# Linear attention with a gated block: the reciprocals of the heads' sums go through DRAM to q's rows

## The chip, the core and the metric

The kernel runs on one core of one Trainium2 chip. The metric is the time of one execution on the device, in microseconds (us). A TensorE (PE) does the products, VectorE (DVE), ScalarE (ACT) and GpSimd (POOL) do the rest; most transfers are issued from the queue of SyncE (SP), a few from POOL's. PSUM tiles hold products, SBUF tiles hold operands, DRAM holds inputs, outputs and scratch.

## The reference

S = 2048 rows, D = 576, 32 heads of 18 columns, an inner width of 4608 in the gated block. All is in f32.

```python
xn = layernorm(x)
q, k, v = heads(xn @ wqkv)                  # 32 heads of 18
phi = lambda t: where(t > 0, t + 1, exp(t)) + 1e-6
kv  = einsum("bhsd,bhse->bhde", phi(k), v)
z   = sum over s of phi(k)                  # the key sums
den = einsum("bhqd,bhd->bhq", phi(q), z) + 1e-6
o   = einsum("bhqd,bhde->bhqe", phi(q), kv) / den
s   = o @ wo
g   = silu((gelu(xn @ w_gate) * (xn @ w_up)) @ w_down)
out = x + s * g
```

## The kernel before

The rows are cut into four blocks of 512 (`TBN`), numbered `tb` = 0 to 3, and each block into four tiles of 128 (`TT`). An operand that must keep f32 precision is held as a high and a low word in f32r, and a product is several passes over those words (`PASSES`).

Stage 1 (to about 183 us): `kv_tile(t)` runs over the sixteen row tiles. It makes k, v and the last 64 columns of q for one tile in three products (`x_mm(t, 0)`, `(t, 1)`, `(t, 2)`), applies phi, and adds to the accumulators of kv and of the key sums (`kv_mm(t - 1)`). `q_turn(t)` turns those columns of q of two tiles with PE and copies them into `ph4[tb]`. The products q of blocks 0 and 1 lie in the middle of this stage (`q_store`): their phi is stored in DRAM (`ph_d`), to be loaded later (`q_load`).

Stage 2 (about 183 to 290 us) is the place of the change. q's columns are laid out in five groups: four groups `gi` of seven heads (126 columns and two columns that belong to the last head), and a fifth with what is left. Before the change it goes so:

- `q_hold(2, 7, ...)` and `q_hold(3, 8, ...)` do the four q products (14 passes each) of blocks 2 and 3; between them stand the pieces of work in their lists. `kv_done` masks kv; `kv_wo(gi)` multiplies kv by wo, so that s = phi(q) @ (kv wo) / den. The same product has two more columns of wo, one of ones, that give the key sums; `kv_wo` spreads them over heads into `zc`. `move_rows` copies the two odd rows into their places, with small copies from SBUF to SBUF.
- `den(tb)`: twenty products (in two passes each) of phi(q) with `zc` give the sums of the 32 heads for 512 rows, then 1e-6 is added and the reciprocal taken, on DVE; four ACT and four DVE steps put it as high and low words into `rd`.
- `scale(tb, ...)`: the reciprocals must stand on the rows of phi(q), 18 rows for each head. For each of the five groups, one product of the 0/1 matrix `sel` with `rd` puts them there in PSUM, and DVE multiplies phi(q) by it. `make_sel` and `copy_sel` make the matrix beforehand on POOL and ACT.
- `halve(tb, ...)`: high word on ACT, low word on DVE.
- `s_mm(tb, t)`: 28 passes make one row tile of s, ACT copies it, SP stores it in DRAM (`s_d`).

The tiles of s run in the order of blocks 2, 3, 0, 1; the table `aside` names the work after each tile: den, scale and halve of the next block, `build` of operands of the next stage (T1 to T4), `load_mat(0)` of the first weights and `back(...)`, which reads back other operands (B11, T2, T1) by POOL's queue. Nearly every instruction is pinned in program order on its engine (`pin`), DMA issues too, so each engine's list, SP's included, is the order of the code.

Stage 3 (about 290 to 1085 us) makes the gate and up products in matrices, and stage 4 the down products and the end.

Buffers are named slots: `big(i, ...)`, `mid(i, ...)`; a later tile in the same slot waits for the last use of the earlier one. `bank` gives one of six PSUM banks, `own_bank` one of two, `gl_tile` one of six SBUF tiles of 512 columns, `tmp` one of four.

Of the kernel before, what the change touches and what calls it, by code (L numbers as in the profile page):

```python
# [15 lines left out]
P = 128  # L16
# [39 lines left out]
def block_kernel(ctx, tc, x, xe, xt_d, wq_d, wkv0_d, wkv1_d, wkv2_d, wo, wgu_d, wd_d, out):  # L56
# [330 lines left out]
    pkv, pks, vas, es, pqt, ph4, ph, ph_d = ({} for _ in range(8))  # L387
# [69 lines left out]
    def q_turn(t):  # L457

        tb, i = divmod(t, TT)
        b = bank(f"qx_{t}")  # L460
        for n in range(2):
            pin(nc.tensor.transpose(b[:, n * P : (n + 1) * P], pqt.pop(t + n)[:, 0:2], ident))
        if i == 0:
            ph4[tb] = gl_tile([P, TBN], f"ph4_{tb}")
            if tb < 2:
                ph_d[tb] = dr.tile([P, NHG, TBN], F32, name=f"phd_{tb}")
        act(ph4[tb][:, i * P : (i + 2) * P], b[:, 0:P2], AF.Copy)
        if i == 2 and tb < 2:
            dma(out=ph_d[tb][:, 4, :], in_=ph4[tb])
# [41 lines left out]

    def q_store(tb, gi):
        o = gl_tile([P, TBN], f"ph_{tb}_{gi}")
        q_mm(tb, gi, o)
        dma(out=ph_d[tb][:, gi, :], in_=o)

# [6 lines left out]
    def ph_of(tb, gi):  # L523
        return ph4[tb] if gi == 4 and tb > 1 else ph[tb][:, gi, :]
# [48 lines left out]
    def load_wo():  # L573

        n = NHG * P
        t = big(14, [P, 2 * n + D + 2], F32, "kvm")
        at["one"] = t[0:H, n + D + 2 :].rearrange("p (g j) -> p g j", g=NHG)
        at["kvm"] = t[:, 0:n].rearrange("p (g j) -> p g j", g=NHG)
        at["wo"] = w = big(12, [P, 4, D + 2], F32, "wo_t")
        at["wo4"] = w4 = t[:, n : n + D + 2]  # L580
# [5 lines left out]
        dma(out=w4[1 : W4 + 1, 0:D], in_=wo[4 * GW : D, :])  # L586

    def kv_wo(gi):
# [8 lines left out]
        zc, mh = at["zc"], at["maskh"]  # L597
# [3 lines left out]
        for c, cs in enumerate((slice(0, HALF), slice(HALF, D + 2))):  # L601
            pw.append(bank(f"kw_{gi}_{c}"))
            mm(
                pw[c][0:wdt, 0 : cs.stop - cs.start], at["kvm"][0:k, gi, 0:wdt], w[0:k, cs],
                start=True, stop=True,
            )
        r, x_ = slice(0, Q4 if gi == 4 else GW), slice(Q4, W4)
        z = pw[1][:, HALF : HALF + 1]
# [6 lines left out]
        if gi == 4:  # L615
            vec("tensor_copy", zx[x_], z[x_])
# [3 lines left out]
        vec("tensor_scalar", zc[r, gi, :], mh[r, gi, :], z[r], None, op0=ALU.mult)  # L620
# [5 lines left out]
    def move_rows():  # L626
        for gi in range(4):
            r, e = slice(Q4 + 2 * gi, Q4 + 2 * gi + 2), slice(GW, P)
            dma(out=at["zc"][e, gi, H - 1 : H], in_=zx[r])
# [3 lines left out]
    def make_sel():  # L633

        n = NHG * P
        buf = big(15, [P, n + TBN], F32R, "aux")
        at["sel"] = sel = buf[:, 0:n].rearrange("p (g j) -> p g j", g=NHG)
        at["rd"] = rd = buf[:, n : n + TBN]
        one = at["one"]
        pool("memset", one, 1.0)  # L640
        four, last = one[:, 0:4, 0:GW], one[:, 4, :].rearrange("p (r j) -> p r j", r=2)
        for o, pattern, base in ((four, [[GW, 4], [1, GW]], 0), (last, [[0, 2], [1, Q4]], 4 * GW)):
            pool(
                "affine_select",
                out=o, in_=o, compare_op=ALU.is_ge, fill=0.0, base=base,
                pattern=pattern, channel_multiplier=-DH,
            )
            pool(
                "affine_select",
                out=o, in_=o, compare_op=ALU.is_ge, fill=0.0, base=DH - 1 - base,  # L650
                pattern=[[-s_, n_] for s_, n_ in pattern], channel_multiplier=DH,
            )
        pool(
                "affine_select",
            out=one[:, 0:4, GW:P], in_=one[:, 0:4, GW:P], compare_op=ALU.is_ge, fill=0.0,
            base=1 - H, pattern=[[0, 4], [0, P - GW]], channel_multiplier=1,
        )
        pool("memset", rd.bitcast(F32), 0.0)

    def copy_sel():  # L660
        one, sel = at["one"], at["sel"]
        for i in range(4):
            r = slice(i * H, (i + 1) * H)
            if i % 2:
                act(sel[r], one, AF.Copy)
            else:
                pool("tensor_copy", sel[r], one)

    HB = TBN // 4

    def den(tb):

        pd = bank(f"d_{tb}")
        for gi in range(NHG):
            for i in range(4):
                mm(
                    pd[H * i : H * (i + 1), 0:HB], at["zc"][:, gi, :],
                    ph_of(tb, gi)[:, i * HB : (i + 1) * HB],
                    start=(gi == 0), stop=(gi == NHG - 1),
                )  # L680
        r = gl_tile([P, HB], f"r_{tb}")
        rd = at["rd"]
        vec("tensor_scalar", r, pd[:, 0:HB], EPS, None, op0=ALU.add)
        vec("reciprocal", r, r)
        for i in range(4):
            c, rows, low = slice(i * HB, (i + 1) * HB), slice(H * i, H * (i + 1)), i ^ 1
            act(rd[rows, c], r[rows], AF.Copy)
            vec("tensor_sub", rd[H * low : H * (low + 1), c], r[rows], rd[rows, c].bitcast(F32))

    pqs, s_d, words = {}, {}, {}  # L690

    def scale(tb, *gs):

        for gi in gs:
            pb = bank(f"b_{tb}_{gi}")
            mm(pb, at["sel"][:, gi, :], at["rd"], start=True, stop=True)
            p = ph_of(tb, gi)
            vec("tensor_mul", p, p, pb)

    def halve(tb, *gs):  # L700

        if tb % 2 and gs[0] == 0:
            words[tb] = [big(i, [P, 4, TBN], F32R, f"pq_{tb}_{i}") for i in (12, 14)]
        for gi in gs:
# [7 lines left out]
            else:  # L712
                if tb % 2:
# [575 lines left out]
    for n in range(N0, 2 * N0):  # L1289
# [13 lines left out]
        if n == 2 * N0 - 2:  # L1303
            after.append(make_sel)
        if n == 2 * N0 - 1:
            after += [copy_sel, lambda: difference(1, 1), lambda: difference(1, 2)]
        kv_tile(n, early, middle, ends, after)

    q_hold(2, 7, [
        [lambda: kv_mm(2 * N0 - 1), kv_done, lambda: difference(1, 3)],  # L1310
        [lambda: q_turn(2 * N0 - 2), lambda: kv_wo(4)],
        [lambda: kv_wo(0), lambda: kv_wo(1), move_rows],
        [lambda: kv_wo(2), lambda: kv_wo(3)],
    ])
    q_hold(3, 8, [
        [lambda: den(2)],
        [lambda: scale(2, 0, 1), lambda: halve(2, 0, 1)],
        [lambda: scale(2, 2, 3), lambda: halve(2, 2, 3)],
        [lambda: scale(2, 4), lambda: halve(2, 4)],
    ])  # L1320
# [7 lines left out]
    def first_matrix():  # L1328
# [5 lines left out]
    q_load(0, 7)  # L1334
    aside = {
        (2, 0): [lambda: den(3), lambda: build(1, "T1", X_SLOT["T1"])],
        (2, 1): [lambda: scale(3, 0, 1), lambda: halve(3, 0, 1)],
        (2, 2): [lambda: scale(3, 2, 3, 4), lambda: halve(3, 2, 3, 4)],
        (2, 3): [lambda: build(1, "T3", X_SLOT["T3"]), lambda: load_mat(0), lambda: q_load(1, 8)],
        (3, 0): [lambda: den(0), lambda: build(1, "T2", X_SLOT["T2"])],  # L1340
        (3, 1): [lambda: scale(0, 0, 1), lambda: halve(0, 0, 1), lambda: back("B11")],
        (3, 2): [lambda: scale(0, 2, 3, 4), lambda: halve(0, 2, 3, 4)],
        (3, 3): [lambda: build(1, "T4", X_SLOT["T4"]), lambda: back("T2")],
        (0, 0): [lambda: den(1), lambda: mat_sums(0)],
        (0, 1): [lambda: scale(1, 0, 1), lambda: halve(1, 0, 1)],
        (0, 2): [lambda: scale(1, 2, 3, 4), lambda: halve(1, 2, 3, 4)],
        (0, 3): [lambda: back("T1")],
# [4 lines left out]
    for tb in (2, 3, 0, 1):  # L1352
# [82 lines left out]
```

## Time and profile before

| | |
|---|---|
| median of 3 runs | 1492.87 us (1492.6 to 1493.64) |
| the profiled execution | 1492.91 us, span 1491.2 us |
| granted TensorE clock | 1.000 |
| PE busy | 1481.9 us, 99% of the span |
| DVE, ACT, POOL busy | 71%, 38%, 36% |
| HBM | 174 GB/s over the span |

All the profile's times come from the one profiled execution and count from its first instruction. A row of the timeline or of the chain gives start, length, engine, what was written and what was read; "x14" counts instructions. A row of the windows view gives the stretch, its length, the busy time (and count) of PE, PEld (weight loads), DVE, ACT and POOL, then the granted clock, the DMA share and GB/s. A row of grouped instructions gives line, engine, operation, out<-in and shapes, count, then the summed busy time and the mean in ns, then the idle time before them. SPq is SP's queue of DMA issues: the length there is that of the issue, not of the transfer.

### The profile page before, as it was taken

Reading aid. Unit: us, or ns where it says so; the run is one execution under the profiler, and the core shown is the slowest. Engines: PE = TensorE matmul, PEld = TensorE weight load, DVE = VectorE, ACT = ScalarE, POOL = GpSimd, SP = SyncE. Lnnn points to the kernel's source line nnn. Section 1 sums busy time; section 2 is a strip of 40 time slices with the busy share of each in tenths; the row PEclk is TensorE's granted clock in tenths of the full one; section 3 lists DMA queues with packets and bytes.
Section 4 is the critical chain, followed back from the end, with each engine's and each line's share of the span. In section 5 each row is a group of like instructions: output and inputs, shape, how many; then the busy total and the mean of one; then the engine's idle time right before and its main releaser. Section 6 shows DMA issues by size and latency. Waiting matters only on the chain.

```text
span 1491.2 us, 22334 instructions
## 1 busy us (share of the span) xinstructions
PE 1481.9 (99%) x8355; PEld 1327.8 (89%) x8355; DVE 1063.9 (71%) x1586; ACT 560.9 (38%) x1043; POOL 543.6 (36%) x521
## 2 busy tenths in 40 slices
PE   9999999999999999999999999999999999999998
PEld 8989989988888888888888888888899999999998
DVE  7667577377788787788787778787785575555775
ACT  5535445332232232332222322223445454445443
POOL 5442431144665544565554565554310020001120
PEclk9999999999999999999999999999999999999999
DMA  6355015533443423444433344333697766686873
GB/s 238 131 213 180 1 43 194 206 149 132 165 173 144 162 106 132 149 174 152 157 119 122 143 173 171 138 134 119 216 335 252 235 215 220 226 292 217 299 253 113
DMA packets 114614, 260.67 MB, mean 175 GB/s; under 512 B 10234, under 2 KB 38778, under 8 KB 112458
## 3 DMA queue, kind: packets, MB, share of 16 engines
q1 hardware_dynamic: 112730, 249.95, 46.7%
q0 software_dynamic: 1632, 8.91, 1.6%
q8 instruction: 65, 1.06, 0.3%
q10 hardware_dynamic: 144, 0.39, 0.1%
q14 instruction: 43, 0.35, 0.1%
HBM read 161.27 MB, written 97.91 MB: 174 GB/s over the span
## 4 chain that ended last, share of the span: by engine, by line
PE 94%; DVE 2%; DMA 2%; ACT 1%; issue 0%; POOL 0%; SPq 0%; ACTq 0%; DVEq 0%; POOLq 0%
PE bd L1010 27%; PE al L804 15%; PE ga L804 15%; PE de L804 15%; PE be L804 8%; PE kv L93 6%; PE s L93 4%; PE q L93 2%; DMA kept_T<-xo_T 1%; PE kv_a L93 1%; ACT xo_T L87 0%; DMA xf_B<-in_xt_dram 0%; PE d L93 0%; PE kw L93 0%; DVE xo_T L90 0%
## 5 line engine op out<-in xcount | busy, mean ns | idle before, releaser
L1010 PEld LDWEIGHTS bd<-t,s 128*128 128x128 f32 x3024 | 400.9, 188 | 0.1
L1010 PE MATMUL bd<-t,s 128*128 128x288 f32 x3024 | 401.0, 295 | 0.0
L90 DVE TENSOR_TENSOR s<-sr,s 128x512 fp32r<-128x512 f32 x252 | 176.1, 739 | 119.8 <-ACT s L87 117.8
L87 ACT ACTIVATE s<-sr 128x512 fp32r<-128x512 f32 x252 | 149.1, 626 | 189.0 <-PE bd L1010 131.0
L96 POOL TENSOR_TENSOR hs<-h,h 128x512 f32<-128x512 f32 x68 | 94.7, 1401 | 203.8 <-DVE h L90 201.1
L87 ACT ACTIVATE h<-h 128x512 f32<-128x512 f32 x108 | 67.1, 633 | 244.5 <-POOL sm L96 123.1
L96 POOL TENSOR_TENSOR sx<-sx 128x288 f32<-128x288 f32 x24 | 27.9, 1180 | 322.9 <-DVE sx L90 321.8
L93 PE MATMUL kv<-wkv,xo_B 128*128 128x416 f32 (+1 forms) x672 | 129.9, 349 | 0.0
L93 PEld LDWEIGHTS kv<-wkv,xo_B 128*128 128x128 f32 x672 | 121.4, 188 | 1.3 <-POOL wkv L96 0.2
L90 DVE TENSOR_TENSOR wa<-raw,wa 128x256 fp32r<-128x256 f32 x72 | 79.2, 1100 | 50.8 <-ACT wa L87 47.5
L96 POOL TENSOR_TENSOR sm<-raw 128x384 f32<-128x384 f32 x72 | 75.8, 1053 | 107.1 <-DMA raw<-in_wgu_dram 86.5
L90 DVE TENSOR_TENSOR h<-h,u 128x512 f32<-128x512 f32 x108 | 95.7, 886 | 3.7
L87 ACT ACTIVATE wa<-sm 128x1152 fp32r<-128x1152 f32 x36 | 41.8, 1161 | 135.8 <-PE de L804 135.8
L90 DVE TENSOR_TENSOR wa<-sm,wa 128x768 fp32r<-128x768 f32 x72 | 63.1, 877 | 36.9 <-ACT wa L87 36.1
L96 POOL TENSOR_TENSOR td<-td 128x288 f32<-128x288 f32 x72 | 70.1, 973 | 53.0 <-DMA td<-in_wd_dram 48.7
L90 DVE TENSOR_TENSOR wb<-raw,wb 128x256 fp32r<-128x256 f32 (+1 forms) x108 | 72.0, 666 | 7.3 <-ACT wb L87 5.8
L90 DVE TENSOR_TENSOR wb<-sm,wb 128x256 fp32r<-128x256 f32 x72 | 61.3, 852 | 20.6 <-ACT wb L87 20.0
L87 ACT ACTIVATE u<-al 128x512 f32<-128x512 f32 x72 | 40.9, 592 | 88.4 <-PE al L804 88.4
L90 DVE TENSOR_TENSOR u<-u,ga 128x512 f32<-128x512 f32 x72 | 49.3, 686 | 19.9 <-PE ga L804 19.3
L804 PE MATMUL al<-xo_B,wa 128*128 128x512 f32 x252 | 63.0, 389 | 0.0
L804 PE MATMUL be<-xo_T,wa 128*128 128x512 f32 x252 | 63.0, 389 | 0.0
L804 PE MATMUL be<-xr_T,wa 128*128 128x512 f32 x252 | 63.0, 389 | 0.0
(175 smaller groups left out, 2773.4 us busy)
## 6 DMA issues: line engine op xcount, KB each, us to landing
sr<-hs SPq DMA_DIRECT2D x252, 256.0 KB
hs<-h SPq DMA_DIRECT2D x68, 512.0 KB
raw<-in_wgu_dram SPq DMA_DIRECT2D x36, 768.0 KB
hs<-hs SPq DMA_DIRECT2D x102, 256.0 KB
td<-in_wd_dram SPq DMA_DIRECT2D x18, 576.0 KB
td<-td SPq DMA_DIRECT2D x18, 576.0 KB
tr<-td SPq DMA_DIRECT2D x16, 576.0 KB
tr<-in_wd_dram SPq DMA_DIRECT2D x12, 576.0 KB
```

The source lines that it names most:

```text
L87: pin(nc.scalar.activation(*args, **kw))
L90: pin(getattr(nc.vector, op)(*args, **kw))
L93: pin(nc.tensor.matmul(*args, **kw))
L96: pin(getattr(nc.gpsimd, op)(*args, **kw))
L804: nc.tensor.matmul(o, w[0:rows, wi, :], xop[0:rows, xi, :], start=(start and n == 0), stop=(n == len(PASSES) - 1), skip_group_check=True,)
L1010: nc.tensor.matmul(banks[j][:, 0:HALF], hw[n, s][:, a, t * P : (t + 1) * P], w[:, c, g % 4], start=(new and g == 0 and m == 0), stop=(g == ...
```

## The change

The products with `sel` go, and with them `make_sel`, `copy_sel` and the words in `rd`. `den_end` stores the reciprocals of a block in DRAM (`rd[tb]`, 32 heads x 512), and `to_rows(tb)` copies them from there into an SBUF tile `rb[tb]` in the layout of phi(q), by nine transfers whose source repeats: four of 7 heads x 18 rows, one of two rows for four groups, and for the fifth group two of 3 heads x 18 rows and two of one head x 10 rows. `scale` multiplies by `rb`. There is one slot for `rb` (15), which the four blocks use in turn.

The key sums come from five products of two columns (`key_sums`), placed ahead of kv times wo. Blocks of s run in the order 0, 2, 3, 1: block 0 is loaded first, block 3 is stored and loaded again instead of held. `den` of block 0 lies between the q products of block 2, that of block 2 between those of block 3, that of block 3 is spread in five parts (`den_mm`) up to behind the first tile of s. `q_turn` in a row tile moves from behind the second product to behind the third.

```diff
@@ kv_tile
         x_mm(t, 1)
-        if t % 2 == 0 and t % (2 * TT):
-            q_turn(t - 2)
...
         x_mm(t, 2)
         run(list(middle))
+        if t % 2 == 0 and t % (2 * TT):
+            q_turn(t - 2)
@@ q_mm
-        phi(o, pq, f"q{tb}_{gi}", tb % 2 == 1)
+        phi(o, pq, f"q{tb}_{gi}", tb > 0)
@@ new
+    def key_sums():
+        pz = bank("z")
...
+            mm(
+                pz[0:wdt, 2 * gi : 2 * gi + 2], at["kvm"][0:k, gi, 0:wdt], w[0:k, D : D + 2],
+                start=True, stop=True,
+            )
+        x_ = slice(Q4, W4)
+        vec("tensor_copy", zx[x_], pz[x_, 8:9])
+        for gi in range(NHG):
...
+            vec("tensor_scalar", zc[r, gi, :], mh[r, gi, :], z, None, op0=ALU.mult)
+        for gi in range(4):
+            dma(out=zc[GW:P, gi, H - 1 : H], in_=zx[Q4 + 2 * gi : Q4 + 2 * gi + 2])
@@ den
+    def den_end(tb):
+        r = gl_tile([P, HB], f"r_{tb}")
+        vec("tensor_scalar", r, dens[tb][:, 0:HB], EPS, None, op0=ALU.add)
+        vec("reciprocal", r, r)
+        rd[tb] = dr.tile([H, TBN], F32, name=f"rd_{tb}")
+        dma(out=rd[tb].rearrange("h (i c) -> i h c", i=4), in_=r)
...
+    def to_rows(tb):
+        rb[tb] = o = big(15, [P, NHG, TBN], F32, f"rb_{tb}")
+        def heads(rows, gi, h, n, k):
+            src = rd[tb][h : h + n, None, :].to_broadcast([n, k, TBN])
+            dma(out=o[rows : rows + n * k, gi, :], in_=src)
+        for gi in range(4):
+            heads(0, gi, HG * gi, HG, DH)
+        src = rd[tb][H - 1 : H, None, :].to_broadcast([2, 4, TBN])
+        dma(out=o[GW:P, 0:4, :], in_=src)
+        for r in (0, Q4):
+            heads(r, 4, 4 * HG, 3, DH)
+            heads(r + 3 * DH, 4, H - 1, 1, Q4 - 3 * DH)
@@ scale
-            pb = bank(f"b_{tb}_{gi}")
-            mm(pb, at["sel"][:, gi, :], at["rd"], start=True, stop=True)
             p = ph_of(tb, gi)
-            vec("tensor_mul", p, p, pb)
+            vec("tensor_mul", p, p, rb[tb][:, gi, :])
@@ the order of stage 2
+    q_load(0, 7)
+    q_hold(2, 8, [
+        [lambda: kv_mm(2 * N0 - 1), kv_done],
+        [key_sums, lambda: q_turn(2 * N0 - 2), lambda: difference(1, 3)],
+        [lambda: den(0), lambda: to_rows(0), lambda: kv_wo(4)],
+        [move_rows, lambda: kv_wo(0), lambda: kv_wo(1)],
     ])
+    behind = [
+        [lambda: kv_wo(2), lambda: scale(0, 0, 1), lambda: halve(0, 0, 1)],
+        [lambda: kv_wo(3), lambda: den(2), lambda: scale(0, 2, 3), lambda: halve(0, 2, 3),
+         lambda: den_mm(3, 4, ph4[3], True, False), lambda: den_mm(3, 0, pg[0], False, False)],
+        [lambda: scale(0, 4), lambda: to_rows(2), lambda: halve(0, 4),
+         lambda: den_mm(3, 1, pg[1], False, False)],
+        [lambda: q_load(3, 7), lambda: den_mm(3, 2, pg[2], False, False)],
+    ]
+    for gi in range(4):
+        q_store(3, gi)
+        run(behind[gi])
...
+        (0, 0): [lambda: den_mm(3, 3, pg[3], False, True), lambda: den_end(3),
+                 lambda: build(1, "T1", X_SLOT["T1"])],
+        (0, 1): [lambda: scale(2, *five), lambda: halve(2, *five), lambda: to_rows(3),
+                 lambda: q_load(1, 8)],
+        (0, 3): [lambda: build(1, "T3", X_SLOT["T3"]), lambda: load_mat(0)],
+        (2, 0): [lambda: build(1, "T2", X_SLOT["T2"])],
+        (2, 1): [lambda: scale(3, *five), lambda: halve(3, *five), lambda: back("B11")],
+        (2, 2): [lambda: den(1), lambda: to_rows(1)],
+        (2, 3): [lambda: build(1, "T4", X_SLOT["T4"]), lambda: back("T2")],
+        (3, 0): [lambda: mat_sums(0)],
+        (3, 1): [lambda: scale(1, *five), lambda: halve(1, *five)],
+        (3, 3): [lambda: back("T1")],
```

More of the change, by code (lines that the diff above doesn't have):

```diff
@@ L386, in block_kernel @@
     left = {}
-    pkv, pks, vas, es, pqt, ph4, ph, ph_d = ({} for _ in range(8))
+    pkv, pks, vas, es, pqt, ph4, ph, ph_d, pg = ({} for _ in range(9))
     def x_mm(t, c, passes=None, new=bank):
@@ L464, in q_turn @@
             ph4[tb] = gl_tile([P, TBN], f"ph4_{tb}")
-            if tb < 2:
+            if tb != 2:
                 ph_d[tb] = dr.tile([P, NHG, TBN], F32, name=f"phd_{tb}")
         act(ph4[tb][:, i * P : (i + 2) * P], b[:, 0:P2], AF.Copy)
-        if i == 2 and tb < 2:
+        if i == 2 and tb != 2:
             dma(out=ph_d[tb][:, 4, :], in_=ph4[tb])
@@ L523, in ph_of @@
     def ph_of(tb, gi):
-        return ph4[tb] if gi == 4 and tb > 1 else ph[tb][:, gi, :]
+        return ph4[tb] if gi == 4 and tb == 2 else ph[tb][:, gi, :]
     def q_load(tb, i):
@@ L575, in load_wo @@
         n = NHG * P
-        t = big(14, [P, 2 * n + D + 2], F32, "kvm")
-        at["one"] = t[0:H, n + D + 2 :].rearrange("p (g j) -> p g j", g=NHG)
+        t = big(14, [P, n + D + 2], F32, "kvm")
         at["kvm"] = t[:, 0:n].rearrange("p (g j) -> p g j", g=NHG)
         at["wo"] = w = big(12, [P, 4, D + 2], F32, "wo_t")
-        at["wo4"] = w4 = t[:, n : n + D + 2]
+        at["wo4"] = w4 = t[:, n:]
         for t in (w, w4[:, None, :]):
@@ L586, in load_wo @@
         dma(out=w4[1 : W4 + 1, 0:D], in_=wo[4 * GW : D, :])
+    def key_sums():
+        pz = bank("z")
+        zc, mh = at["zc"], at["maskh"]
+        for gi in range(NHG):
+            wdt, k = (W4, W4 + 1) if gi == 4 else (GW, GW + 1)
+            w = at["wo4"] if gi == 4 else at["wo"][:, gi]
+            mm(
[4 more added lines that the diff above has]
+        vec("tensor_copy", zx[x_], pz[x_, 8:9])
+        for gi in range(NHG):
+            r = slice(0, Q4 if gi == 4 else GW)
+            z = pz[r, 2 * gi : 2 * gi + 1]
+            vec("tensor_scalar", zc[r, gi, :], mh[r, gi, :], z, None, op0=ALU.mult)
+        for gi in range(4):
+            dma(out=zc[GW:P, gi, H - 1 : H], in_=zx[Q4 + 2 * gi : Q4 + 2 * gi + 2])
     def kv_wo(gi):
@@ L600, in kv_wo @@
         pw = []
-        for c, cs in enumerate((slice(0, HALF), slice(HALF, D + 2))):
+        for c in range(2):
+            cs = slice(c * HALF, (c + 1) * HALF)
             pw.append(bank(f"kw_{gi}_{c}"))
             mm(
-                pw[c][0:wdt, 0 : cs.stop - cs.start], at["kvm"][0:k, gi, 0:wdt], w[0:k, cs],
+                pw[c][0:wdt, 0:HALF], at["kvm"][0:k, gi, 0:wdt], w[0:k, cs],
                 start=True, stop=True,
@@ L628, in move_rows @@
             r, e = slice(Q4 + 2 * gi, Q4 + 2 * gi + 2), slice(GW, P)
-            dma(out=at["zc"][e, gi, H - 1 : H], in_=zx[r])
             for t, i in ((at["kvh"], 2), (at["kvl"], 3)):
                 dma(out=t[e, gi, :].bitcast(F32), in_=at["kv4"][r, i, :].bitcast(F32))
[L633 to L646, printed above, removed]
-            )
[L648 to L669, printed above, removed]
+    HB = TBN // 4
+    rd, rb, dens = {}, {}, {}
+    def den_mm(tb, gi, src, first, last):
+        if first:
+            dens[tb] = own_bank(f"d_{tb}")
+        for i in range(4):
+            mm(
+                dens[tb][H * i : H * (i + 1), 0:HB], at["zc"][:, gi, :],
+                src[:, i * HB : (i + 1) * HB], start=first, stop=last, skip_group_check=True,
+            )
@@ L681, in den @@
[L681 to L688, printed above, removed]
+            den_mm(tb, gi, ph_of(tb, gi), gi == 0, gi == NHG - 1)
+        den_end(tb)
@@ L1302, in block_kernel @@
             after.append(lambda: difference(1, 0))
-        if n == 2 * N0 - 2:
-            after.append(make_sel)
         if n == 2 * N0 - 1:
-            after += [copy_sel, lambda: difference(1, 1), lambda: difference(1, 2)]
+            after += [lambda: difference(1, 1), lambda: difference(1, 2)]
         kv_tile(n, early, middle, ends, after)
[L1309 to L1313, printed above, removed]
-    ])
[L1315 to L1320, printed above, removed]
+    q_load(0, 7)
[4 more added lines that the diff above has]
+        [move_rows, lambda: kv_wo(0), lambda: kv_wo(1)],
+    ])
+    behind = [
[9 more added lines that the diff above has]
+        run(behind[gi])
     X_BACK = {"B11": 13, "T2": 7, "T1": 8, "T3": 12, "B21": 4, "B22": 5, "T4": 6}
@@ L1330, in first_matrix @@
         return mat_pieces(0)
-    q_load(0, 7)
+    five = range(NHG)
     aside = {
[L1336 to L1347, printed above, removed]
+        (0, 0): [lambda: den_mm(3, 3, pg[3], False, True), lambda: den_end(3),
[10 more added lines that the diff above has]
+        (3, 3): [lambda: back("T1")],
         (1, 0): [lambda: pieces.extend(first_matrix()), lambda: run(pieces[0])],
@@ L1351, in block_kernel @@
     pieces = []
-    for tb in (2, 3, 0, 1):
+    for tb in S_ORDER:
         for t in range(TT):
```

18 lines of the change are left out of this document (5 added, 13 removed).

## The prediction

> **What bounds the kernel now.** I read the page's shares first, then the chain of waits, then who waited for whom on PE, then the stage between 183 and 290 us in the chain's order of time.
>
> ```profile
> span 1491.2 us, 22334 instructions
> PE 1481.9 (99%) x8355; PEld 1327.8 (89%) x8355; DVE 1063.9 (71%) x1586; ACT 560.9 (38%) x1043; POOL 543.6 (36%) x521
> ...
> PE 94%; DVE 2%; DMA 2%; ACT 1%; issue 0%; POOL 0%; SPq 0%; ACTq 0%; DVEq 0%; POOLq 0%
> ```
>
> PE is busy for 99% of the span and is 94% of the chain that ended last. So an instruction taken from PE is time won, and a wait put into PE's list is time lost, one for one. The granted clock is 1.00 in every stretch quoted below, so the clock plays no part. In the stretch 120 to 300 us, the waits on PE are two:
>
> ```profile
> PE qx L462 <- POOL w_q L96: 1.1, 1, 1.1
> PE b L93 <- DVE aux L90: 0.2, 1, 0.2
> ```
>
> The stage itself, from the chain (start, length, what):
>
> ```profile
> 187.54 3.26 PE q L93 x14
> 190.80 0.22 PE qx L462 x2
> 191.02 0.97 PE kw L93 x4
> 192.00 3.20 PE q L93 x14
> 195.20 1.95 PE kw L93 x8
> ...
> 205.50 1.23 PE d L93 x40
> ...
> 210.14 0.47 PE b L93 x2
> ...
> 227.26 3.72 PE s L93 x28
> 230.98 0.69 PE b L93 x3
> ```
>
> A q product group takes 3.20 us, a den 1.23, a tile of s 3.72, and a reciprocal product b 0.23 (0.47/2, 0.69/3). DVE, ACT and POOL hide beside these.
>
> **What leaves PE.** Twenty products b go: 20 x 0.23 = 4.6 us. The 0.2 us wait before one of them goes too. q_turn moves behind the third x_mm of its tile, over 2 us later, longer than the 1.1 us that PE waited there for POOL; after it PE does kv_mm of the tile before, which had no wait. So 1.1 us goes.
>
> **What PE gains.** key_sums issues five products with two columns, f32, so ten passes. The trace has no such product. The passes of den cost 1.23/40 = 0.03 us, those of kw 1.95/8 = 0.24; so 0.3 to 2.4 us. I take 0.11 a pass, as in the two narrow transposes qx (0.22/2): 1.1 us. kw loses two columns of 290: nothing. den's products are the same number in other places. Sum on PE: -4.6 - 0.2 - 1.1 + 1.1 = -4.8 us. The dropped make_sel, copy_sel and the sixteen small aux steps lay on POOL, ACT and DVE under PE's work; they are worth nothing by themselves.
>
> **Waits that the change adds.** First, den(0) needs the key sums, which the four two-row copies carry into zc:
>
> ```profile
> 192.83 0.71 SPq L99 DMA_DIRECT2D small<-eps_t  x1
> ...
> 195.02 0.56 SPq L99 DMA_DIRECT2D small<-eps_t  x1
> ...
> 217.86 0.37 SPq L99 DMA_DIRECT2D ph<-phd  x1
> ```
>
> In the new PE list q(2,1) ends at 190.8 (old time scale), key sums end at 191.9, qx and q(2,2) at 195.3. The sums reach zx at about 192.1; four issues of at most 0.71 us end at 195, and den reads the groups in the same order. I put 0 for this wait, with 1 us as upper end.
>
> Second, and decisive: the new transfers. rb is 128 rows x 5 groups of 2 KB, sent four times. What transfers cost here:
>
> ```profile
> 143.00:144.00 1.00, 1.00 (x8) 1.00 (x7) 1.00 (x2) 0.10 (x1) 0.00 (x0) 1.00 0.88 341
> 218.80:222.90 4.10, 4.05 (x61) 3.46 (x59) 1.32 (x3) 1.35 (x3) 1.29 (x1) 1.00 0.84 322
> 222.90:223.10 0.20, 0.20 (x2) 0.20 (x3) 0.14 (x1) 0.00 (x0) 0.00 (x0) 1.00 0.00 0
> 223.20:223.90 0.70, 0.70 (x8) 0.70 (x7) 0.67 (x2) 0.00 (x0) 0.00 (x0) 1.00 1.00 392
> ```
>
> These are stretches of the windows view; the last two columns are the busy share of the 16 DMA engines and GB/s. Line two is ph's load of 1.31 MB, issued at 217.86, landed at 222.9: about 1 us of start, 4.1 of moving. Line four is a store of an s tile in rows of 2.3 KB: 392/16 = 24.5 GB/s an engine, so 84 ns for 2 KB. Line one is wo's load of 126 rows at full flow: 0.88 of the engines, and 14/16 = 0.875. Fourteen is the largest number up to 16 that divides 126, so I read it as rows dealt in equal shares, with two engines left out.
>
> A group copy of the change has 126 rows on the SBUF side, but its source is 7 rows in DRAM, each repeated 18 times. Bounds: if the 126 decides, 14 engines work; if the 7 has to be dealt in equal shares too, 7 do. I take 7, since 14 cannot share out 7 rows; likewise 3 engines for the copies of 54 rows from 3, and 2 for the two-row one. The busiest engine then moves 4 x 18 + 2 x 18 + 4 + 2 = 114 packets of 2 KB, 114 x 84 ns = 9.6 us per block of s. With 14 (and 9) engines it is 4 x 9 + 2 x 6 + 4 + 2 = 54, or 4.5 us, and the nine issues at 0.56 to 0.71 us make it 5.
>
> The Trainium skill, page "DMA: Bandwidth & Descriptors", section "Why a DMA increments its semaphore by 16 and not by 1", says that a transfer runs on the largest number up to 16 that divides the slowest dimension (not of size 1) of both sides; its section "Rules for kernel authors" warns that an outermost dimension of size c < 16 confines a transfer to c engines. The 0.88 agrees for 126 against 126; no run here shows a repeated source. By the page it is 7 engines and the slower sum; by the 126 rows alone it is the faster one, my first rival.
>
> Now the SP queue of the new kernel, in order: the store of q(3,2); nine rb(2) copies; the store of q(3,3); the load of ph(3), which reads these stores; an s store; the store of rd(3); an s store; nine rb(3) copies, which read rd(3); the load of ph(1). PE's den(1), after s(2,2), waits for that load. I take it that what is issued from SP runs in this order on each engine, so the load of ph(1) ends behind all of it.
>
> PE's own clock, without waits: from 190.8, products up to the end of q(3,2) add 1.1 + 0.2 + 4 x 3.20 + 2 x 1.23 + 0.97 + 1.95 + 2 x 0.98 + 0.5 (two fifths of den, 3) and one more q of 3.20, so 216.0. s(0,0) begins at 216.0 + 3.20 + 0.5 = 219.7; den(1) comes after seven s tiles and 0.25 of den(3): 246.0.
>
> The queue's clock needs the evacuation of q(3,2):
>
> ```profile
> L90 DVE TENSOR_TENSOR ph<-ph,b 128x512 f32<-128x512 f32 x20 | 12.7, 683 | 2.2 <-PE b L93 2.1
> ...
> L96 POOL TENSOR_TENSOR ph<-ph,e_q 128x512 f32<-128x512 f32 x8 | 10.3, 1289 | 20.9 <-DVE ph L90 11.9 <-DVE small L90 5.9 <-ACT e_q L87 3.0
> ...
> L87 ACT ACTIVATE e_q<-e_q 128x512 f32<-128x512 f32 x8 | 5.1, 632 | 9.9 <-DVE e_q L90 9.8
> ...
> L90 DVE RECIPROCAL r<-r 128x128 f32<-128x128 f32 x4 | 3.8, 953 | 0.1
> ...
> L87 ACT ACTIVATE e_q<-q 128x512 f32<-128x512 f32 x4 | 2.4, 599 | 3.5 <-PE q L93 3.5
> ```
>
> Relu 0.60, exp 0.63, sum 1.29: the store of q(3,2) goes out at 218.6, the first rb(2) copy at 219.0, its data at 220.2. Then: 9.6 of copies, 229.8; the store of q(3,3) behind them on the same engines, 8 packets of 84 ns, 230.5, and up to 0.5 until SP may issue; load ph(3) 5 us, 236.0; an s store 0.75 and rd(3) 1.3 (64 KB in 512 B pieces on few engines: 0.7 by bytes, 2.7 at 84 ns for each of 32; I stay near the bytes), 238.1; then 0.4 + 1.0 until rb(3) moves, 9.6 of copies: 249.1. ph(1)'s share of an engine, 80 KB at up to 27 GB/s, 3.05 more: 252.2. There is a further guest:
>
> ```profile
> 239.99 0.70 POOL L99 DMA_DIRECT2D xr_B<-kept_B  x1 [19.72 <-ACT s L87]
> ```
>
> The read of B11 starts after T3 as it does now, near 240, and takes its own 3.05 us of every engine: 255.2. So PE waits 255.2 - 246.0 = 9.3 us at den(1) (6.2 if B11 doesn't collide).
>
> Third: the same for s(1,0). den(1) ends at 256.5, the reciprocal at 257.8. Behind ph(1) the engines still hold five s stores (0.75 each) and the 768 KB of the first gate weights (1.8): 260.8; T2's read, 3.05: 263.8; rd(1) 1.3, then 1.4, then 9.6: 276.1. The last of the five multiplications and the first rest, 0.68 each, give 277.5. PE wants it at 256.5 + 5 x 3.72 + 0.5 = 275.6. Wait: 1.9 us.
>
> Elsewhere I put nothing: rb(0) lands near 211 and its last use before s(0,0) is at 218, hidden by q(3,0) to q(3,2), 9.6 us of PE; rb(2) lands at 229.8 and its halves are done at 234, just before s(2,0) at 234.8, hidden by s(0,0) to s(0,3); without that cover each us is one lost. Multiplying by rb in SBUF instead of PSUM stays at about 0.69, as the neighbouring subtractions in SBUF. What follows, the gate and up stage, starts from weights and xr tiles that are still early by 5 us or more.
>
> **Sum.** -4.8 + 9.3 + 1.9 = +6.4 us. The profiled execution took 1492.9 us around its span of 1491.2, and the median of the runs is 1492.87, so the forecast is 1499.3 us.
>
> **Rivals.** (a) Fourteen engines, faster. At 5 us a block, both block copies in the queue's clock are 4.6 us shorter: ph(1) is there by 246.0, and nothing else waits. 1492.9 - 4.8 = 1488.1. It decides where a block's copies take less than about 5 us; the wait is nearly back in the gain (zero sum) at 7.3. For it: 14 engines are what 126 rows showed. Against: 7 source rows. (b) The copies are as slow as I say, but the queue overlaps better (no collision with B11, stores not in line): wait 3 to 6 us, s(1,0) none: 1491 to 1494, which can't be told from now. (c) Copies slower still, say 16 us a block, because one engine reads the same DRAM row 18 times: den(1) then waits 22 us, s(1,0) 6 to 8 more: about 1517. Nothing in the trace shows it. That the products stay is no case: scale has no mm any more.
>
> **Numbers.** The forecast's case 0.65 (its own range 1495.5 to 1504: wait at den(1) 6.2 to 12, at s(1,0) 0 to 3), (a) 0.21, (b) 0.10, (c) 0.04. A measurement of this kernel can tell about 0.2%, 3 us, from no change. Faster is (a) with a little of (b): 0.22. Within 0.2% is the rest of (b): 0.09. Slower is the forecast and (c): 0.69. The range has to take in most of (a): 1487.5 to 1504.
>
> **What would show it.** In the profile after: no group b on PE; rows of rb with a DMA share near 0.4 (7/16) while they alone move; PE idle before a d group with 20 products (40 passes) near 245 to 255, ended by the DMA of ph from phd; a smaller wait in s near 276; q_turn's wait gone. I am wrong if the share goes to 0.8 while rb moves, or if no wait stands before the last den; if den(0) or s(0,0) waits instead, the mechanism is right and the place wrong.

## The result, and the profile after

| | before | after |
|---|---|---|
| median of 5 runs | 1492.87 us (1492.6 to 1493.64) | 1509.28 us (1508.14 to 1510.26) |
| ratio | | 1.0108, 95% interval 1.0094 to 1.0123 |
| the profiled execution | 1492.91, span 1491.2 | 1509.93, span 1508.2 |
| mean granted clock | 1.000 | 0.995 |

The change makes the kernel 16.4 us slower. The forecast was 6.4 us slower, with 1504.0 us as the upper end of its range: the sign and the main mechanism were right, and the size was 10 us short.

The page's shares of after, and the chain that ended last. PE was 94% of that chain before; it is 84% now, and transfers are 6%:

```profile
span 1508.2 us, 22335 instructions
...
PE 1481.7 (98%) x8345; PEld 1326.1 (88%) x8345; DVE 1054.7 (70%) x1566; ACT 556.4 (37%) x1029; POOL 541.1 (36%) x512
...
PE 84%; DMA 6%; DVE 2%; ACT 1%; SPq 1%; issue 1%; POOL 1%; DVEq 0%; ACTq 0%; POOLq 0%
```

Who waited for whom on PE, over the whole run (total, times, longest):

```profile
PE d L93 <- DMA ph<-phd: 13.1, 1, 13.1
PE s L93 <- DVE pq L90: 1.9, 1, 1.9
...
PE kv L93 <- DVE xo_B L90: 1.5, 2, 1.0
PE mr L194 <- DVE mv L90: 1.1, 1, 1.1
PE d L93 <- POOL ph L96: 0.8, 1, 0.8
...
PE kv_a L93 <- POOL va L96: 0.3, 1, 0.3
```

The first two lines are the two waits of the forecast, at the places that it named: the group d is den(1), behind s(2,2). The forecast put 9.3 and 1.9 us there. The lines of kv, mr and kv_a are in stage 1, where it expected none; the 1.1 us at qx and the 0.2 us at b are gone.

The chain of waits from the last copy of block 2 to s(1,0):

```profile
230.08 7.05 DMA rb<-rd
...
238.55 7.19 DMA rd<-r
...
245.80 0.77 SPq L99
...
246.62 8.88 DMA rb<-rd
...
255.57 8.30 DMA ph<-phd
...
264.00 2.39 PE d L93 x40
...
267.80 6.08 DMA rd<-r
...
279.86 6.66 DMA rb<-rd
...
287.98 4.12 PE s L93 x29
```

It reads as the forecast's queue: a copy of rb(2); rd(3)'s store, 7.19 us for 64 KB; a copy of rb(3), 8.88; the load of ph(1), 8.30; den(1). Between 230 and 288 us there is nothing of PE in it but the den itself.

The windows view (last three columns: granted clock, DMA share, GB/s) while rb(0) moves, with only small copies beside it, and while PE idles before den(1):

```profile
206.00:207.00 1.00, 1.00 (x6) 0.82 (x5) 1.00 (x3) 0.31 (x2) 0.64 (x1) 1.00 0.45 147
208.00:209.00 1.00, 1.00 (x6) 0.78 (x6) 0.00 (x0) 0.00 (x0) 0.00 (x0) 1.00 0.43 139
...
215.00:216.00 1.00, 1.00 (x30) 0.76 (x22) 1.00 (x3) 0.97 (x3) 0.00 (x0) 1.00 0.19 66
216.00:217.00 1.00, 1.00 (x6) 0.84 (x5) 0.92 (x2) 0.91 (x3) 0.30 (x1) 1.00 0.02 7
...
251.00:253.00 2.00, 0.00 (x0) 0.00 (x0) 0.00 (x0) 0.00 (x0) 0.00 (x0) 1.00 0.44 163
253.00:255.00 2.00, 0.00 (x0) 0.00 (x0) 0.00 (x0) 0.00 (x0) 0.00 (x0) 0.60 0.48 180
255.00:257.00 2.00, 0.00 (x0) 0.00 (x0) 0.00 (x0) 0.00 (x0) 0.00 (x0) 0.50 0.56 170
...
260.00:262.00 2.00, 0.00 (x0) 0.00 (x0) 0.70 (x3) 0.63 (x1) 0.00 (x0) 0.50 0.94 351
...
264.00:266.00 2.00, 2.00 (x40) 1.91 (x40) 1.09 (x2) 0.71 (x2) 0.54 (x1) 0.50 0.98 390
266.00:268.00 2.00, 2.00 (x18) 1.71 (x11) 1.25 (x2) 0.00 (x0) 0.00 (x0) 0.74 0.87 288
268.00:270.00 2.00, 2.00 (x17) 2.00 (x16) 0.00 (x0) 0.00 (x0) 0.00 (x0) 1.00 0.96 362
```

Seven engines of sixteen are 0.44, and the share is 0.43 to 0.47 while the first copies of rb(0) move; its last copies, from three source rows, run at 0.19 (3/16) until about 215.7. PE stands still from 251 to 264; up to 257 about half of the engines stand still too (0.44 to 0.56), and after that the load of ph(1) and what is issued behind it fill them (0.94). The clock goes to 0.50 in this idle time and is still there when PE resumes, so den(1) takes 2.39 us in place of 1.23. That was in no step of the forecast.

### The profile page after: what moved, and what is told of

The parts are those of the page before. It is cut to its first block, busy times and chain, and to the rows that moved or that the text cites. A ratio compares the mean times of both kernels' runs of the same rounds, so it can differ in the third digit from the quotient of the medians.

```text
span 1508.2 us, 22335 instructions
## 1 busy us (share of the span) xinstructions
PE 1481.7 (98%) x8345; PEld 1326.1 (88%) x8345; DVE 1054.7 (70%) x1566; ACT 556.4 (37%) x1029; POOL 541.1 (36%) x512
## 4 chain that ended last, share of the span: by engine, by line
PE 84%; DMA 6%; DVE 2%; ACT 1%; SPq 1%; issue 1%; POOL 1%; DVEq 0%; ACTq 0%; POOLq 0%
PE bd L1010 26%; PE al L804 15%; PE de L804 15%; PE ga L804 15%; PE be L804 8%; PE kv L93 3%; DMA rb<-rd 2%; SPq L99 1%; DMA kept_T<-xo_T 1%; DMA rd<-r 1%; PE s L93 1%; DMA rq<-in_wq_dram 1%; DMA ph<-phd 1%; PE q L93 0%; DMA xf_B<-in_xt_dram 0%
## 5 line engine op out<-in xcount | busy, mean ns | idle before, releaser
L804 PE MATMUL al<-xr_B,wa 128*128 128x512 f32 x252 | 63.0, 389 | 0.0
```

Of the source, the lines that this page charges most:

```text
L804: nc.tensor.matmul(o, w[0:rows, wi, :], xop[0:rows, xi, :], start=(start and n == 0), stop=(n == len(PASSES) - 1), skip_group_check=True,)
```

## Experiments

All kernels were timed against the kernel before, on the same chip, whose median was 1492.9 to 1493.4 us. The changed kernel is called "after" here.

### What the copies cost in all

```diff
@@ to_rows(tb)
+        if tb:
+            rb[tb] = rb[0]
+            return
         rb[tb] = o = big(15, [P, NHG, TBN], F32, f"rb_{tb}")
```

> The changed kernel with the copies done for block 0 alone: its reciprocals are used for all four blocks, so 27 of the 36 copies are left out. Theory (copies of rb cost the waits): PE waits below 1 us at den of block 1 and at s of block 1, the clock stays at 1.00, 1491 to 1494 us; what is left above the prediction's gain of 4.8 us is the 3.7 us of stage 1 and 1 to 2 us of small waits before 225 us. Rival (the loads of ph, the operand reads and the stores of rd fill the engines by themselves): den of block 1 still waits 4 us or more, 1497 us or more.

Measured: 1492.75 us (ratio 0.9998, 0.9989 to 1.0006), clock 1.00. No wait at den(1) or s(1,0); on PE there remain, beside the start of the kernel:

```profile
PE kv L93 <- DVE xo_B L90: 1.6, 2, 1.0
PE mr L194 <- DVE mv L90: 1.0, 1, 1.0
...
PE d L93 <- POOL ph L96: 0.3, 1, 0.3
PE kv_a L93 <- POOL va L96: 0.2, 1, 0.2
```

So 27 of the 36 copies, with the waits that they set off, cost 1509.28 - 1492.75 = 16.5 us; the forecast's two waits made 11.2. The rival falls: loads of ph, operand reads and rd's stores do not fill the time by themselves. And with the copies out of the way the change gains nothing, where its PE terms promised 4.8 us. Most of that is lost in stage 1, which comes next.

### Stage 1: where q_turn's move cost 2.6 us

In the timelines the last kv_a product of stage 1 starts at 182.09 us before and at 184.69 after, though PE's own work up to there is the same. Two kernels try the move alone: after with q_turn put back, and before with q_turn moved.

```diff
@@ kv_tile (after, q_turn back; the other kernel has the reverse edit in before)
         x_mm(t, 1)
+        if t % 2 == 0 and t % (2 * TT):
+            q_turn(t - 2)
...
         x_mm(t, 2)
         run(list(middle))
-        if t % 2 == 0 and t % (2 * TT):
-            q_turn(t - 2)
```

> The changed kernel with q_turn in a row tile put back behind the second product, as it was before the change. Theory (the move delays POOL and the stores and reads of operands behind it, and PE waits for those in stage 1): the last kv_a product comes at about 182.1 us in place of 184.7, PE waits 1.1 us again at a qx, and the time falls by 2.6 us to about 1506.7. Rival (the 2.6 us come from chance in the transfers or from another part of the change): within 0.5 us of 1509.3.

> The kernel before, with nothing changed but q_turn in a row tile moved behind the third product. Theory (the move costs 2.6 us in stage 1): about 1495.5 us, with waits of PE for xo_B and mv that the kernel before has not. Rival (the prediction's step: the wait of 1.1 us at qx goes and nothing takes its place): about 1491.8 us.

Measured: before with the move, 1496.05 us, ratio 1.0017 (1.0008 to 1.0026), 2.7 us slower than before, as the theory says; the waits for xo_B (1.6 us) and mv (1.2) are there. After with q_turn back is 1508.93 us (1505.77 to 1510.45), only 0.35 below after and inside its spread. The trace of its profiled execution (1510.45 us) shows why the 2.6 us do not appear there. Stage 1 did become shorter, by 2.3 us from one kv_a (65.80) to the last (183.63; after: 64.60 and 184.69). But the profiled run began 1.2 us late, and a wait of 1.8 us at s(1,0), shorter than the 1.9 in after, was followed by a halved clock, which after had not:

```profile
284.24:287.65 3.41, 1.61 (x13) 1.38 (x12) 2.07 (x5) 2.01 (x6) 0.00 (x0) 1.00 0.16 62
287.65:291.06 3.41, 3.41 (x17) 3.41 (x16) 1.79 (x3) 0.56 (x2) 0.57 (x1) 0.50 0.44 173
```

PE works at half speed for 3.4 us, up to 291, which is 1.7 us lost. So this kernel decides little by its time, and neither 1506.7 nor its rival is shown by it; the other one decides.

The cause is in SP's and ACT's timelines, first before, then after:

```profile
54.20 0.34 SPq L99 DMA_DIRECT2D phd<-ph  x1
54.64 0.38 SPq L99 DMA_DIRECT2D x<-in_x_dram  x1
55.07 0.98 SPq L99 DMA_DIRECT2D kept_B<-xo_B  x2
61.26 0.38 SPq L99 DMA_DIRECT2D rq<-in_wq_dram  x1
...
68.28 0.83 ACT L87 ACTIVATE wq<-rq 128x768 fp32r<-128x768 f32 x1
```

```profile
57.43 0.34 SPq L99 DMA_DIRECT2D phd<-ph  x1
57.88 1.42 SPq L99 DMA_DIRECT2D x<-in_x_dram  x1
59.34 0.94 SPq L99 DMA_DIRECT2D kept_B<-xo_B  x2
61.50 0.38 SPq L99 DMA_DIRECT2D rq<-in_wq_dram  x1
...
71.62 0.85 ACT L87 ACTIVATE wq<-rq 128x768 fp32r<-128x768 f32 x1 [3.25 <-DMA rq<-in_wq_dram]
```

q_turn issues one store, phd<-ph, and it stands in SP's queue ahead of a load of x, two stores of kept_B (1.31 MB each) and the load rq. Moved, it is ready 3.2 us later; the kept_B stores start 4.3 us later and are still moving when rq is issued, and rq lands 3.3 us later for ACT. From there POOL's wq, the build of xo_T, its store and the next xf_B are late, up to PE's waits for xo_B. The last experiment on it moves q_turn as the change does and takes only this store out of the way. It was made on the best kernel of the last section below, whose q_turn stands in the old place. The edit beside the move is:

```diff
@@ q_turn
-        if i == 2 and tb != 2:
+        if i == 2 and tb not in (0, 2):
             dma(out=ph_d[tb][:, 4, :], in_=ph4[tb])
@@ kv_tile, at its end
+        if t == TT + 1:
+            dma(out=ph_d[0][:, 4, :], in_=ph4[0])
```

> The kernel with the clear queue (1489.95 us), with q_turn moved behind the third product as in the change, but the one store of its result that stood ahead of the kept_B stores and the load rq on SP's queue now issued behind that load. Theory (what q_turn's move costs in stage 1 comes from this store: it is ready 3.2 us later, at 57.4 us in place of 54.2, and SP holds back the two kept_B stores and rq behind it): rq lands in time for ACT's step wq at about 68.3 us, no wait for xo_B or mv, the wait at qx gone, 1488.6 to 1489.4 us. Rival (the later place of the two transposes on PE and of their copy on ACT costs it): wq on ACT at 71 us or later, waits for xo_B and mv of over 2 us in sum, 1492 to 1493 us.

Measured: 1489.98 us against 1489.95, so the move costs nothing any more, and it gains nothing either: the wait of 1.1 us at qx is gone, and 0.9 us at mr for mv takes its place. So the store is shown for the waits for xo_B (1.6 us where only q_turn moved, none here), and the rival, over 2 us of waits from the transposes' later place, falls. The wait for mv stays with the store out of the way, so it belongs to the move itself; the expected gain of about 1 us is missed by it. rq is in time: ACT's wq starts at 69.70 in a run that began 1.4 us late.

### Seven engines or fourteen

```diff
@@ den_end
-        rd[tb] = dr.tile([H, TBN], F32, name=f"rd_{tb}")
-        dma(out=rd[tb].rearrange("h (i c) -> i h c", i=4), in_=r)
+        rd[tb] = dr.tile([H, 2, TBN], F32, name=f"rd_{tb}")
+        for k in range(2):
+            dma(out=rd[tb][:, k, :].rearrange("h (i c) -> i h c", i=4), in_=r)
@@ to_rows
-            src = rd[tb][h : h + n, None, :].to_broadcast([n, k, TBN])
+            src = rd[tb][h : h + n].rearrange("h k c -> (h k) c")[:, None, :].to_broadcast([2 * n, k // 2, TBN])
...
-        src = rd[tb][H - 1 : H, None, :].to_broadcast([2, 4, TBN])
+        src = rd[tb][H - 1, :, None, :].to_broadcast([2, 4, TBN])
```

> The changed kernel, with each head's reciprocals stored twice in DRAM (two stores of 64 KB instead of one), so that a group copy has a source of 14 rows, each repeated 9 times, in place of 7 rows repeated 18 times. Theory (the source's row count sets how many DMA engines share a copy): the busiest engine moves 68 packets in place of 114, 5.7 us a block in place of 9.6; the DMA share while the copies of block 0 move alone rises from 0.45 to over 0.6 (then the nine issues of 0.75 us set the pace); PE's wait in front of den of block 1 falls from 13.1 us to 5 to 7, the granted clock sags less there, and the time is 1499 to 1504 us. Rival (the copies are slow because the same DRAM rows are read again and again, or because of their nine issues): share stays at 0.45, wait at 12 to 14, time 1509 to 1511 us.

Measured: 1504.27 us, ratio 1.0077 (1.0064 to 1.009), 5 us faster than after and just past the slow end of the theory. The windows view while rb(0) moves:

```profile
207.00:208.00 1.00, 1.00 (x6) 0.81 (x5) 0.10 (x1) 0.00 (x0) 0.00 (x0) 1.00 0.76 246
208.00:209.00 1.00, 1.00 (x6) 0.83 (x5) 0.00 (x0) 0.00 (x0) 0.00 (x0) 1.00 0.75 242
209.00:210.00 1.00, 1.00 (x6) 0.78 (x5) 0.26 (x1) 0.86 (x2) 0.00 (x0) 1.00 0.76 289
```

The share is 0.76 in place of 0.45 (fourteen engines of sixteen would be 0.88). The landings of the first copy of rb(0) that the traces record are plainer: leaving out one that stands right behind the issue in both, seven in after (206.77 to 207.39 us) and fourteen here (207.39 to 208.04). So the number of source rows sets the number of engines of these copies. By the rule cited in the prediction from the Trainium skill, page "DMA: Bandwidth & Descriptors", section "Why a DMA increments its semaphore by 16 and not by 1", it would be 7 and 14; the trace agrees. But the wait at den(1) fell only to 11.2 us, not to 5 to 7: rd(3) still took 8 us from issue to rb(3)'s first copy, the copies met the read of B11, and the load of ph(1) was issued only when one of them had landed (a copy of 9.60 us in its chain). SP's transfers use eight semaphores in turn, and each is issued only when the eighth before it has landed: here that copy at 252.99 us and the load at 253.06, in after 255.50 and 255.57. This hold lies in the kernel, and what it costs was not tested. Faster copies are worth what the queue behind them lets through.

### The order of the queue

Two edits move one transfer each: the load of ph(1) ahead of rb(3)'s copies, and the read of B11 four tiles later, from behind tile (2,1) of s to behind (3,1) (the text of the expectation counts five).

```diff
@@ aside, first kernel
-        (0, 1): [..., lambda: to_rows(3), lambda: q_load(1, 8)],
+        (0, 1): [..., lambda: q_load(1, 8), lambda: to_rows(3)],
@@ aside, second kernel
-        (2, 1): [..., lambda: back("B11")],
+        (2, 1): [...],
...
-        (3, 1): [...],
+        (3, 1): [..., lambda: back("B11")],
```

> The changed kernel with the load of ph of block 1 issued ahead of the nine copies of rb of block 3. Theory (den of block 1 waits only because its load stands behind these copies on SP's queue): the wait of 13.1 us there goes to below 1, the clock stays at 1.00 there, and the copies, now later, let s of block 3 wait 4 to 9 us instead; 1498 to 1505 us. Rival (the transfers together are too much for the time, whatever their order): the first tile of s of block 3 waits 11 us or more, 1507 to 1511 us.

> The changed kernel with the read of B11 issued five s tiles later, behind the halves of block 1. Theory (the copies of rb of block 3 give way to B11's packets between 245 and 249 us, and ph of block 1 comes that much later): PE's wait in front of den of block 1 falls from 13.1 to 9 to 10.5 us, near the prediction's 9.3, the clock still halves in it, and the time is 1505 to 1507 us. Rival (SP's queue is held by the copies' issue and landing whether or not B11 is there): the wait stays above 12 us and the time at 1508.5 or more.

Measured: 1512.24 us (1.0126, 1.0112 to 1.014) and 1513.19 us (1.0131, 1.0117 to 1.0146): both slower than after. In the first, den(1) no longer waits, as expected, and s(3,0) waits 5.6 us, in the theory's range; but s(1,0) waits 6 us too, and the clock halves behind both. The time is past the rival's, though not at the one place that it named:

```profile
260.71 0.85 PE L93 MATMUL s<-kvh,pq 128*128 128x288 f32 x2 [3.71 <-ACT pq L87]
263.90 1.33 PE L93 MATMUL s<-kvh,pq 128*128 128x288 f32 x4 [1.87 <-DVE pq L90]
284.54 0.85 PE L93 MATMUL s<-kvh,pq 128*128 128x288 f32 x2 [3.61 <-ACT pq L87]
288.24 1.33 PE L93 MATMUL s<-kvh,pq 128*128 128x288 f32 x4 [2.38 <-DVE pq L90]
```

In the second, den(1) waits 10.9 us in place of 13.1, so B11's read did cost 2.2 us there (the forecast's sum had 3.05); but in its new place it meets rb(1)'s copies, and s(1,0) waits 5.0. The wait at den(1) is nearer to the theory's, the time on the rival's side, for a reason that neither had. Moving one transfer moves the collision.

### All of it together

The four edits above (two copies in DRAM, q_turn back, load of ph(1) first, B11 late), and the same with one copy in DRAM:

> The changed kernel with four edits together: reciprocals twice in DRAM (14 source rows), q_turn back behind the second product, the load of ph of block 1 ahead of the copies for block 3, the read of B11 five s tiles later. Theory (the change's loss is its transfers and q_turn's place, while taking the products b from PE is worth about 4 us): no wait over 1.5 us in stage 2, the clock at 1.00 throughout, the qx wait of 1.1 to 1.4 us is there, and the time is 1489.5 to 1492.5 us, below the kernel before. Rival (rd's way through DRAM to rb takes so long that some block of s waits in any order): a wait of 3 us or more in front of the first tile of s of block 3 or 1, with the clock halved behind it, and 1495 us or more.

> As the kernel with four edits, but with the reciprocals once in DRAM (7 source rows, 18 repeats). Theory (seven engines make a block's copies 4 us longer than fourteen): the first tile of s of block 3 waits 1 to 4 us, the clock may halve behind it, and the time lies 3 to 8 us above the kernel with four edits, at 1494 to 1500 us. Rival (once the order is mended the copies are hidden at either speed): within 1 us of it.

Measured: 1499.27 us (1.0041, 1.003 to 1.0053) and 1507.87 us (1.0099, 1.0086 to 1.0112). The first meets its rival: in its profiled execution (1503.81 us) s(1,0) waits 7.3 and then 2.2 us, and the clock halves. The two differ by 8.6 us, more than the 3 to 8 expected, so seven engines against fourteen decide much of the loss. What was left was rd(1): its reciprocal came on DVE behind scale and halve of block 3, its store was issued at 257.26 us and the first copy at 266.25. Hence den(1) one tile earlier (this diff and the next in short form):

```diff
-        (2, 1): [scale(3), halve(3)],
-        (2, 2): [den(1), to_rows(1)],
-        (2, 3): [build T4, back("T2")],
-        (3, 1): [scale(1), halve(1), back("B11")],
+        (2, 1): [den(1), scale(3), halve(3), to_rows(1)],
+        (2, 3): [build T4, back("T2", "B11")],
+        (3, 1): [scale(1), halve(1)],
```

> The kernel with four edits, but den of block 1 moved one s tile up, ahead of scale of block 3, its copies right behind the halves of block 3, and the read of B11 behind that of T2. Theory (in the kernel with four edits the reciprocal of block 1 stood on DVE behind scale and halve of block 3, at 256 us, and its store then queued behind reads): rd of block 1 is stored 6 us earlier, its copies meet fewer reads, the first tile of s of block 1 waits 0 to 2 us in place of 9.5, the clock stays at 1.00, 1490 to 1493 us. Rival (the transfers of stage 2 don't fit in its time, in any order): some block of s waits 4 us or more and the time is 1496 us or more.

Measured: 1494.08 us (1.0009, 1.0001 to 1.0018). In the profiled run, its fastest (1491.72), s(1,0) waits 1.6 + 0.3 us and the clock holds; the runs reach to 1499.19, and that one has a mean clock of 0.997, none being lower. The median lies between theory and rival. The last step takes the gate weights and two reads out of rb(1)'s way:

```diff
-        (0, 3): [build T3, load_mat(0)],
-        (2, 1): [den(1), scale(3), halve(3), to_rows(1)],
-        (2, 3): [build T4, back("T2", "B11")],
-        (3, 0): [mat_sums(0)],
+        (0, 3): [build T3],
+        (2, 1): [den(1), scale(3), halve(3), to_rows(1), load_mat(0)],
+        (2, 3): [build T4],
+        (3, 0): [mat_sums(0), back("T2", "B11")],
```

> The kernel with den of block 1 early, and two more transfers taken out of the way of its copies: the load of the first gate weights issued behind these copies, the reads of T2 and B11 behind the sums of these weights. Theory (the 1.9 us that s of block 1 still waited came from rd of block 1 landing 7.6 us after its issue, behind the gate weights, and from copies that ran beside two reads): rd of block 1 lands within 4 us, no wait over 0.5 us in stage 2 but the 1.1 us at qx before it, the clock at 1.00 in every run, 1489.5 to 1491 us, which is below the kernel before by about 0.2%. Rival (the reads, now later, make the gate and up stage wait, or the copies are late for another reason): 1493 us or more, with a wait of 2 us or more in stage 2 or at the start of the gate and up stage.

> The same with the reciprocals once in DRAM, 7 source rows and 18 repeats. Theory (in a queue that is clear, the 4 us that seven engines cost a block are partly hidden): s of block 3 or 1 waits 0 to 3 us, 0 to 5 us above the same kernel with two copies in DRAM. Rival (seven engines cost the same 8 us and more that they cost between the kernels with three and with four edits): 7 us or more above it.

Measured: 1489.95 us, ratio 0.998 (0.9972 to 0.9989), 3.0 us faster than before, and 1497.54 us (1.0028, 1.0017 to 1.004) with one copy in DRAM. The waits on PE of the faster one, beside the start of the kernel:

```profile
PE qx L462 <- POOL w_q L96: 1.4, 1, 1.4
...
PE s L93 <- DVE pq L90: 0.9, 1, 0.9
PE d L93 <- DMA ph<-phd: 0.6, 1, 0.6
```

The median is as expected; the wait of 0.9 us at s is over the 0.5 given, and rd(1) took 5.6 us from issue to the first copy, not 4. The other one shows that seven engines cost 7.6 us even in a clear queue, as the rival said and more than the theory's 0 to 5: den(1) waits 2.7 us, four waits at s make 2.9, and the clock halves once.

## Why the prediction was wrong in size

Two terms of the sum failed: the 1.1 us at qx, which were not won and became a cost of 2.6, and the wait at den(1), which was put at 9.3 us and measured 13.1, with a halved clock behind it that no term had.

- **PE's terms (-4.8).** Right. From start to start in the timelines of before and of the kernel with one block's copies, b took 4.75 us (put at 4.6), the key sums take 0.93 (put at 1.1), den(3) in five parts 0.26 more than in one piece and kw 0.14 more (both put at nothing). That is -3.4 for the -3.5 that the forecast had without waits; the wait of 0.2 us at b is gone too.
- **The step "the 1.1 us at qx goes" failed.** It looked at what follows q_turn on PE and not at the store that q_turn issues. The move cost 2.6 us where 1.1 was to be won: 3.7 of the 10 us that the forecast was short. The kernel with the store moved shows that the 2.6 come through SP's queue, and that the 1.1 are not won without it either: a wait for mv takes the place of the one at qx.
- **den(0).** Its group lasts some 0.35 us longer from start to start than the others, with a small copy of the sums ahead of it in the chain; inside the bound of 1.
- **Seven engines.** Right in number; the price of a block was too low. The packets of rb(0) move from 204.9 to 215.7 us, 10.8 us where 9.6 was worked out for the busiest engine. Rival (a), fourteen engines, is out for this kernel; made true by another layout in DRAM it is worth 5.0, 8.6 or 7.6 us, depending on what else waits.
- **The term of den(1) was undersized: 13.1 for 9.3.** From the first issue of rb(2) to the landing of ph(1) the forecast's clock has 255.2 - 219.0 = 36.2 us; measured are 263.87 - 224.04 = 39.8. The copies of rb(2), beside a store of q, took 13.1 us from first issue (224.04) to the last landing (237.13) against 10.8. From there to the landing of rd(3) it is 8.6 against 8.3, and on to that of ph(1) 18.1 against 17.1. The neighbours in the queue do not explain the 2.3 us at rb(2): rb(0), with only small copies beside it, took 12.8 (203.25 to 216.05). So the block's own price was low, and why a block takes more than its packets' sum was not tested. The forecast's range for this wait, 6.2 to 12, left out what was measured. The collision with B11 was counted, and is there.
- **The clock.** "The clock plays no part" was taken from a trace without long waits. A wait of 13 us halves it: 1.2 us on den(1) and some tenths behind it.
- **s(1,0).** 1.92 us for 1.9, in part by luck: rd(1) landed 6.1 us after its issue where the sum had 7.3, and its copies took 12.6 us from first issue to last landing where it had 11.0. T2's read, which the sum puts in this line, was not tested apart.
- **The rest of 1 us** is what the kernel with one block's copies lost beside stage 1 (1492.75 - 1488.1 = 4.65, less 3.7). The 0.35 in den(0) and a wait of a d for POOL (0.3 us there, 0.8 in after), which the forecast had not, are part of it; what remains stays open.

In sum: 3.7 in stage 1, 16.5 - 11.2 = 5.3 from the copies (3.8 more wait at den(1), and some 1.5 by the halved clock), and about 1 elsewhere make the 10 us. Rival (b), an overlap that makes the queue better than its sum, went the other way; (c), 1517 us, was not reached.

## What to carry to other kernels

When a step moves, list what it issues as well as what it computes: one store, ready 3 us later at the head of a queue, was worth more than the wait that the move removed. A transfer whose source repeats few rows uses few engines; a second copy in DRAM, at the price of one small store, gave twice the engines. Price a block of transfers from its first issue to its last landing (12.8 us here), not by the packets of its busiest engine (9.6), and after moving a transfer, look at which it meets in its new place.

## What was not expected of the hardware

The granted clock halves behind a wait of PE. In after it is back 3.0 us after PE resumes; in the kernel with q_turn back it halves 0.6 us after PE has resumed, for 3.4 us. There a wait of 1.80 us was enough, while 1.92 us in after cost no clock. The traces tell why. Within one execution the changes of the clock lie whole multiples of 3.41 us apart: in after at 253.40 and 267.05, in the other kernel at 253.52, 267.17, 287.65 and 291.06. Counted from these points, each span falls into stretches of 3.41 us. The wait of 1.80 us lies in one stretch, the first of the two lines shown for it above (PE busy for 1.61 of 3.41 us). The one of 1.92 us in after is split, 1.46 and 0.45 us:

```profile
284.12:287.53 3.41, 1.95 (x15) 1.72 (x13) 2.65 (x5) 2.59 (x5) 0.00 (x0) 1.00 0.38 146
287.53:290.94 3.41, 2.96 (x22) 2.96 (x23) 2.89 (x5) 1.66 (x5) 0.00 (x0) 1.00 0.48 188
```

Over all fourteen profiled executions, from 20 us on, the clock halved behind every stretch at full clock in which PE stood idle for 1.80 us or more, and behind none with 1.75 us or less; in the first 9 us of three of them 1.46 us was enough. So near 2 us a wait costs its length or nearly twice it, by where it falls among these stretches, and these lie elsewhere in each execution. The Trainium skill, page "TensorE: Matmul & The Clock Gate", section "Part 1: The HAM clock gate", says that the clock drops after an idle window of about 3.4 us and comes back after a busy one, in windows that run free of the kernel. The traces agree on the 3.4 us and on windows that run free. They do not agree that a whole window must be idle: 1.80 us without PE work sufficed here.
